# HGRN2 scan and SiLU MLP in one kernel: two w_out pieces staged in w_in's staging tiles, and 38 more idle matmuls in the opening

## The chip, the cores and the metric

The kernel runs on one core of a Trainium2 chip. The metric is the device time of one execution in microseconds (us). Before the change the median of 7 runs is 189.18 us (188.8 to 190.96).

A core has five engines that run side by side and wait for one another by semaphores: TensorE (PE, matmuls; its weight loads are listed apart as PEld), VectorE (DVE), ScalarE (ACT), GpSimd (POOL) and SyncE (SP), which here only issues DMA transfers. Each engine works through its own instructions in order.

## The reference

For 4 batches, 8 heads, 768 steps and a head size of 48, a gated linear attention is computed as a recurrence, and its output goes through a two-layer network with SiLU (model width 384, inner width 2048):

```python
f = 1.0 / (1.0 + np.exp(-f_logit))
for t in range(S):
    state = f[:, :, t, :, None] * state + np.einsum('bhd,bhe->bhde', k[:, :, t], v[:, :, t])
    y[:, :, t] = np.einsum('bhd,bhde->bhe', q[:, :, t], state)
x = y.transpose(0, 2, 1, 3).reshape(B * S, H * D)
h = x @ w_in
out = (h * (1.0 / (1.0 + np.exp(-h)))) @ w_out
```

All inputs and the output are float32 in HBM.

## The kernel before

The 768 steps are cut into 6 chunks of 128, which with 4 batches gives 24 units; a unit is one chunk of one batch with all 8 heads (128 rows of 384 values). Two successive units form a pair. Loads of f, k, q and v bring one unit at a time for the first four units and a pair at a time after that (L485).

A unit goes through these steps. ACT turns f into a logarithm of the gate (e and lf, L492 and L494). PE sums it along the chunk by a triangular matrix (cs, L565 and L569). ACT takes exponentials of the sums (ia, a, al, L572 to L576). POOL and DVE scale k and q by them (L578 and L582, tile qk). PE transposes both (tq, L588), DVE copies them out (L590), PE forms the scores (sc, L599), DVE masks them (L603), PE forms y from scores, v and the running state (L608, L612), DVE casts it (L616), and PE transposes it (L620) into xT. From unit 12 on for q and k, and from unit 15 on for y, DMA transposes replace those on PE. The state is brought forward by L630 (PE), L635 or L637 (DVE) and L641 (POOL). For the network, PE multiplies w_in with xT (m1 for the first 6 units one by one, L529, four blocks j = 0 to 3 of 12 matmuls each; mi for pairs later, L540), ACT applies SiLU into hT (L526, L536), PE multiplies hT with w_out (mo, L551), DVE copies the result (L554 to L559) and a DMA stores it (L562). ACT reloads its function table (L677) whenever it goes from exponentials to SiLU or back.

The weights come in as float32 and are cast to bfloat16 once. w_in is loaded in four pieces into the four staging tiles `ws` (L505), w_out in four pieces into the two staging tiles `wt` (L510), each piece 768 KB with the same number of bytes per partition. A cast (L515 to L520) takes each piece into its place: of w_in, pieces 0, 1 and 2 on POOL and piece 3 on DVE; of w_out, piece 0 and 3 on POOL, 1 on DVE and 2 on ACT. Piece m of w_out is needed by the m-th mo of a unit.

The order on every engine is written out ahead of time. `make_tasks` lists all tasks with durations, priorities and the buffers that they take; `schedule` plays them through a model of the engines and the DMA queue, and the order that comes out is emitted as it stands, with waits added for buffers and data. A buffer is handed from one task to the next by class and slot, and the dictionary `where` (L475 to L478) holds the tile that each task's buffer became.

SP's order in the opening, from its thirteenth load on, is: w_in piece 1, f, w_in piece 2, w_out piece 1, w_in piece 3, k, w_in piece 0, q, w_out piece 0, w_out piece 3, v, f (pair 2), w_out piece 2, and then k, q and v of pair 2 and the loads of the next pairs. The staging tiles of w_in are used once each, in the order of these loads: piece 1 lies in the first, piece 0 in the fourth. Of the two tiles `wt`, one holds w_out piece 1 and then piece 3, the other piece 0 and then piece 2, so the loads of pieces 3 and 2 wait for the casts of pieces 1 and 0.

`idle` looks for gaps of PE in the planned order up to 60 us, and fills each to 75% with matmuls of a zero tile, `blank`, into an idle accumulator bank (`warm`, L652); they compute nothing that is used. The count for a gap is worked out in one line:

```python
n = int(best[0] * cfg["idle_fill"] / (0.0565 if out else 0.113))
```

Of the kernel before, what the change touches and what calls it, by code (L numbers as in the profile page):

```python
# [38 lines left out]
    idle_to=60.0,  # L39
    idle_gap=0.2,  # L40
    idle_fill=0.75,
    hold_exp=0,
    hold_silu=1.23,
    keep_exp=161.0,
# [331 lines left out]
def planned(cfg, slots):  # L376

    tasks, T = make_tasks(cfg)
    schedule(tasks, slots, cfg, cfg["margin"])
    fixed = {e: sorted([t for t in tasks if t.eng == e], key=lambda t: (t.start, t.idx)) for e in ENGINES}  # L380
    schedule(tasks, slots, cfg, 0.0, fixed=fixed)
    order = sorted(tasks, key=lambda t: (t.start, t.idx))
    return order, idle(order, slots, cfg)


def idle(order, slots, cfg):

    held = {s: [] for s in range(slots["mlp"])}
    banks = {}
    for t in order:  # L390
        for x in t.acq + t.use:
            if x.cls == "mlp":
                lo, hi = banks.get(x, (t.start, t.end))
                banks[x] = (min(lo, t.start), max(hi, t.end))
    for x, (lo, hi) in banks.items():
        held[x.slot].append((lo, hi + 0.3))
    out, prev = [], cfg["idle_from"]
    for t in [t for t in order if t.eng == "PE"]:
        lo, hi = prev, t.start - cfg["idle_gap"]
        prev = t.start + t.dur  # L400
        if t.start > cfg["idle_to"]:
            break
        best = (0.0, 0.0, 0)
        for s, spans in held.items():
            a = max([lo] + [e for b, e in spans if b < hi])
            if hi - a > best[0] + 1e-6:
                best = (hi - a, a, s)
        n = int(best[0] * cfg["idle_fill"] / (0.0565 if out else 0.113))
        if n > 0:
            out.append((best[1], best[2], n))  # L410
    return out
# [3 lines left out]
def kernel(  # L415
# [15 lines left out]
    d_model, d_ff = moe_w_in.shape  # L431
# [14 lines left out]
        ws=([128, KT, d_ff // CFG["w_pieces"][0]], F32), wt=([128, NT // CFG["w_pieces"][1], d_model], F32),  # L446
# [12 lines left out]
    NI, NO = CFG["w_pieces"]  # L459
# [15 lines left out]
    where = {}  # L475
    for t in tasks:
        for x in t.acq + t.use:
            where[x.key] = buf[x.cls, x.slot]  # L478
    at = lambda *key: where[key]

    def load(x, us):
# [226 lines left out]
```

## Time and profile before

| what | us |
|---|---|
| median of 7 runs (lowest, highest) | 189.18 (188.8, 190.96) |
| the profiled execution | 188.94 |
| its span, from the first to the last instruction | 187.1 |
| PE busy between 9.88 and 20.0 / 20.0 and 30.0 | 8.22 of 10.12 / 6.54 of 10.00 |
| PE busy between 30.0 and 41.3 | 11.30 of 11.30 |
| mean granted clock of PE | 1.000 |

The profile comes from one execution, and its times count from the span's start. A line of a timeline gives start, length, engine, code line, operation, the tile written and the tiles read, shapes, the number of instructions merged, and in brackets the idle time of the engine before it with what ended it. SPq is SP's queue: a line there is the issue of a DMA, whose length is the time that the issue took, and not that of the transfer; the transfer lands later. The chain of work follows the last instruction back to what released it, step by step.

Six lines of the table of DMA issues give the sizes, and the median time from issue to landing:

| load | count | KB each | us to landing |
|---|---|---|---|
| ws from w_in | 4 | 768 | 8.8 |
| wt from w_out | 4 | 768 | 8.0 |
| f, pair | 10 | 384 | 5.5 |
| k, pair | 10 | 384 | 6.1 |
| q, pair | 10 | 384 | 5.8 |
| v, pair | 10 | 384 | 5.3 |

### The profile page before, as it was taken

The page shows a single profiled execution, that of the slowest core. Times are in us where ns is not written, and L with a number is a line of the kernel's source. Part 1 is how long each engine was busy: PE and PEld are TensorE (multiplying, and loading weights), DVE is VectorE, ACT ScalarE, POOL GpSimd, SP SyncE. Part 2 cuts the span into 40 slices and gives each one's busy share as a digit, 9 for nine tenths or more (in the row PEclk, how much of TensorE's full clock was granted, in tenths as well). Part 3 has the DMA queues.
Part 4 walks back from the last instruction along what each step waited for, and adds up shares of the span by engine and source line. Part 5 has one row for each costly group of instructions (what it writes and reads, how often), then busy time and mean ns, then how long its engine had stood idle before and what let it go on. Part 6 is the DMA issues. An engine that isn't in the chain of part 4 may idle for free.

```text
span 187.1 us, 4875 instructions
## 1 busy us (share of the span) xinstructions
PE 174.3 (93%) x2005; PEld 139.3 (74%) x2005; DVE 95.7 (51%) x185; ACT 131.1 (70%) x217; POOL 70.6 (38%) x112
## 2 busy tenths in 40 slices
PE   5998766999999999979999999999999999999991
PEld 4976656777878879768787786678688886966960
DVE  4269435435877773565527736875542415261011
ACT  4443844998797898998988788668669996810810
POOL 2337628444637470552751642490352006000000
PEclk9999999999999999999999999999999999999999
DMA  6999999899999998998999599488776666413101
GB/s 115 220 205 360 373 356 299 238 222 216 223 224 242 190 253 193 230 245 169 226 142 208 126 178 208 80 126 219 158 154 152 141 130 135 100 25 105 42 16 68
DMA packets 120390, 34.22 MB, mean 183 GB/s; under 512 B 116129, under 2 KB 117793, under 8 KB 120369
## 3 DMA queue, kind: packets, MB, share of 16 engines
q1 hardware_dynamic: 119664, 31.76, 77.8%
q0 software_dynamic: 704, 2.16, 3.2%
q8 instruction: 15, 0.25, 0.6%
q14 instruction: 7, 0.05, 0.1%
HBM read 25.17 MB, written 4.72 MB: 160 GB/s over the span
## 4 chain that ended last, share of the span: by engine, by line
PE 70%; SPq 11%; DMA 7%; ACT 5%; issue 2%; POOL 1%; DVE 1%; DVEq 0%; ACTq 0%
PE mlp L551 29%; PE mlp L540 24%; DMA q<-in_q_dram 7%; SPq L485 7%; SPq L505 4%; PE mlp L529 4%; PE sc L599 3%; PE yd L612 2%; PE yd L608 2%; PE cs L565 2%; ACT L677 2%; PE tq L588 1%; PE yd L630 1%; ACT hT L536 1%; PE tq L620 1%
## 5 line engine op out<-in xcount | busy, mean ns | idle before, releaser
L551 PE MATMUL mlp<-w_out,hT 128*128 128x384 bf16 x384 | 69.9, 326 | 0.0
L536 ACT ACTIVATE hT<-mlp 128x512 bf16<-128x512 f32 x72 | 41.7, 597 | 17.4 <-PE mlp L540 14.9
L540 PE MATMUL mlp<-xT,w_in 128*128 128x256 bf16 x432 | 51.5, 273 | 1.1 <-ACT hT L536 1.0
L551 PEld LDWEIGHTS <-hT 128*128 128x128 bf16 x384 | 34.8, 97 | 19.5
L540 PEld LDWEIGHTS <-w_in 128*128 128x128 bf16 x432 | 46.3, 114 | 3.2 <-issue 1.3
L578 POOL TENSOR_TENSOR qk<-k,ia 128x384 bf16<-128x384 f32 x24 | 24.0, 1001 | 51.1 <-ACT al L576 31.2
L603 DVE TENSOR_TENSOR atm<-sc,triu 128x512 bf16<-128x512 f32 x48 | 30.9, 685 | 19.3 <-PE sc L599 19.3
L677 ACT ACT_TABLE_LOAD x23 | 29.5, 1283 | 0.4
L641 POOL TENSOR_TENSOR st<-sd,al 48x192 bf16<-48x192 f32 x40 | 20.9, 522 | 16.1 <-DVE sd L635 8.7
L572 ACT ACTIVATE ia<-cs 128x384 f32<-128x384 f32 x24 | 11.8, 490 | 15.4 <-PE cs L569 10.5
L559 DVE COPY o<-mlp 128x384 f32<-128x384 f32 x22 | 12.2, 556 | 18.0 <-PE mlp L551 14.1
L616 DVE CAST yb<-yd 128x384 bf16<-128x384 f32 x24 | 13.3, 554 | 15.8 <-PE yd L612 15.8
L529 PE MATMUL mlp<-xT,w_in 128*128 128x128 bf16 x288 | 18.7, 220 | 2.0 <-DVE w_in L520 1.6
L582 DVE TENSOR_TENSOR qk<-q,cs 128x384 bf16<-128x384 f32 x24 | 13.2, 550 | 13.8 <-ACT cs L574 8.7
L529 PEld LDWEIGHTS <-w_in 128*128 128x128 bf16 x288 | 16.9, 114 | 2.8 <-DVE w_in L520 1.8
L526 ACT ACTIVATE hT<-mlp 128x512 bf16<-128x512 f32 x24 | 13.6, 597 | 6.8 <-PE mlp L529 6.4
L580 POOL CAST vb<-v 128x384 bf16<-128x384 f32 x24 | 11.6, 506 | 11.0 <-DMA v<-in_v_dram 10.9
L492 ACT ACTIVATE e<-f 128x768 f32<-128x768 f32 (+1 forms) x14 | 10.5, 747 | 5.9 <-DMA f<-in_f_logit_dram 5.8
L635 DVE TENSOR_TENSOR sd<-yd,st 128x384 f32<-128x384 f32 x16 | 8.9, 555 | 8.3 <-PE yd L630 6.2
L574 ACT ACTIVATE cs<-cs 128x384 f32<-128x384 f32 x24 | 11.4, 477 | 0.6
L652 PE MATMUL mlp<-blank 128*128 128x128 bf16 x112 | 10.6, 266 | 1.0 <-DVE blank L657 1.0
L494 ACT ACTIVATE lf<-e 128x768 bf16<-128x768 f32 (+1 forms) x14 | 10.5, 750 | 0.3
(43 smaller groups left out, 149.6 us busy)
## 6 DMA issues: line engine op xcount, KB each, us to landing
f<-in_f_logit_dram SPq DMA_DIRECT2D x10, 384.0 KB, 5.5
k<-in_k_dram SPq DMA_DIRECT2D x10, 384.0 KB, 6.1
q<-in_q_dram SPq DMA_DIRECT2D x10, 384.0 KB, 5.8
v<-in_v_dram SPq DMA_DIRECT2D x10, 384.0 KB, 5.3
ws<-in_moe_w_in_dram SPq DMA_DIRECT2D x4, 768.0 KB, 8.8
wt<-in_moe_w_out_dram SPq DMA_DIRECT2D x4, 768.0 KB, 8.0
out_dram<-o SPq DMA_DIRECT2D x13, 192.0 KB, 2.1
out_dram<-o POOLq DMA_DIRECT2D x11, 192.0 KB, 3.7
```

The lines of the kernel that those rows point to most:

```text
L485: nc.sync.dma_start(out=dst, in_=SRC[x].rearrange("b h s d -> s (b h) d")[c * C:(c + 1) * C, b * H:(b + n) * H])
L526: return nc.scalar.activation(at("hT", P)[:, 4 * j:4 * j + 4, i * C:(i + 1) * C], h, AF.Silu)
L529: nc.tensor.matmul(h[:, r, :], w_tile(kk, 4 * j + r), at("xT", P)[:, kk, i * C:(i + 1) * C], start=(kk == 0), stop=(kk == KT - 1))
L536: return nc.scalar.activation(at("hT", P)[:, 2 * j:2 * j + 2, :], h, AF.Silu)
L540: nc.tensor.matmul(h[:, i, :], w_tile(kk, n), at("xT", P)[:, kk, :], start=(kk == 0), stop=(kk == KT - 1))
L551: nc.tensor.matmul(o, at("hT", P)[:, n, i * C:(i + 1) * C], w_rows(n), start=(n % (NT // 2 if half else NT) == 0), stop=(n == NT - 1 or ha ...
L578: nc.gpsimd.tensor_mul(at("qk", u)[:, 1, :, 0:D], at("k", P)[:, i], at("ia", u))
L582: nc.vector.tensor_mul(at("qk", u)[:, 0, :, 0:D], at("q", P)[:, i], at("cs", u)[:, 0:HD].rearrange("p (h d) -> p h d", d=D))
L603: nc.vector.tensor_mul(at("atm", u)[:, r], at("sc", u)[:, r], triu[:, None, :].to_broadcast([C, NP, C]))
L616: nc.vector.tensor_copy(at("yb", u), at("y", u))
L641: nc.gpsimd.tensor_mul(at("st", u)[lo:lo + D, :, r * D:(r + 1) * D], at("sd", u)[lo:lo + D, :, r * D:(r + 1) * D], at("al", u)[lo:lo + D, ...
L677: nc.scalar.preload_act_table_set(SETS[after[t.idx]])
```

## The change

Two things are changed. First, after the plan is made and the tiles are assigned, w_out pieces 2 and 3 are given other staging tiles: piece 2 is staged where w_in piece 0 lay, and piece 3 where w_in piece 1 lay, both read with the same bytes in another shape. The order on every engine stays as it was. The load of piece 3 now waits for the cast of w_in piece 1 in place of that of w_out piece 1, and the load of piece 2 for the cast of w_in piece 0 in place of that of w_out piece 0. The casts of both pieces read from the new tiles.

Second, two groups of idle matmuls grow: the group ahead of the cs of unit 3 from 6 to 20, and the one ahead of the block j = 3 of m1 of unit 0 from 2 to 26. PE gets 38 matmuls and 38 weight loads more; no other instruction is added or removed.

```diff
@@ CFG
     idle_fill=0.75,
+    idle_more={'cs_3': 14, 'm1_0_3': 24},
     hold_exp=0,
@@ idle
         n = int(best[0] * cfg["idle_fill"] / (0.0565 if out else 0.113))
+        n += cfg["idle_more"].get("_".join(map(str, t.name)), 0) if n else 0
         if n > 0:
             out.append((best[1], best[2], n))
@@ tile_hgrn2_outer__then__act_silu_kernel
             where[x.key] = buf[x.cls, x.slot]
+    for n in range(2, NO):
+        where["wt", n] = where["ws", n - 2].rearrange("p k n -> p (k n)").rearrange("p (n d) -> p n d", d=d_model)
     at = lambda *key: where[key]
```

## The prediction

> **What bounds the kernel now.** I read the page first (busy shares and granted clock), then TensorE's waits, its timeline through the opening, the queue of SyncE (SP), the chain that ended last, and windows over the same stretch.
>
> The page gives TensorE (PE) as the fullest engine, at the full clock in every slice:
>
> ```profile
> PE 174.3 (93%) x2005; PEld 139.3 (74%) x2005; DVE 95.7 (51%) x185; ACT 131.1 (70%) x217; POOL 70.6 (38%) x112
> ...
> PEclk9999999999999999999999999999999999999999
> ```
>
> Its waits over the whole span (total, times, longest):
>
> ```profile
> PE mlp L529 <- DVE w_in L520: 1.6, 1, 1.6
> PE tq L588 <- DVE qk L582: 1.4, 1, 1.4
> PE mlp L540 <- ACT hT L536: 1.0, 1, 1.0
> ```
>
> The first two lie before 29.52 us, the third at 82.56. After 29.52 that third one is the only wait above a tenth of a microsecond: windows give PE 11.30 busy of 11.30 us from 30.0 to 41.3, 40.11 of 40.20 to 81.5, and 100.67 of 100.80 from 82.6 to 183.4. So the kernel is an opening of 29.5 us set by loads, and then a nearly solid row of matmuls. Only two things can shorten it: an earlier start at 29.52, or the little that is left between matmuls after it.
>
> PE's timeline in the opening (start, length, line, count, idle before):
>
> ```profile
> 18.19 0.50 PE L652 MATMUL mlp<-blank 128*128 128x128 bf16 x6
> 19.45 0.32 PE L565 MATMUL cs<-lf,triu 128*128 128x384 bf16 x1 [0.76 <-ACT lf L494]
> ...
> 23.63 0.28 PE L652 MATMUL mlp<-blank 128*128 128x128 bf16 x2
> 25.54 0.86 PE L529 MATMUL mlp<-xT,w_in 128*128 128x128 bf16 x12 [1.63 <-DVE w_in L520]
> ...
> 29.52 0.62 PE L588 MATMUL tq<-ident,qk 128*128 128x128 bf16 x8 [1.45 <-DVE qk L582]
> ```
>
> The idle matmuls of the change go into the first two bracketed waits. The third, at 29.52, stays as it is: it ends when q, issued at 21.11, lands at 28.82. Every SP issue up to 21.64 stands before the changed ones, so I expect the same landing.
>
> SP's queue, with the two re-staged w_out loads (the second of the x2, and the one at 32.66):
>
> ```profile
> 21.64 3.75 SPq L510 DMA_DIRECT2D wt<-in_moe_w_out_dram  x2
> 25.43 0.43 SPq L485 DMA_DIRECT2D v<-in_v_dram  x1
> 25.91 2.03 SPq L485 DMA_DIRECT2D f<-in_f_logit_dram  x1
> 32.66 0.42 SPq L510 DMA_DIRECT2D wt<-in_moe_w_out_dram  x1
> ```
>
> SP stands from 27.94 to 32.66, because the tile it wants is read until then by the cast in GpSimd (POOL). The chain shows what follows:
>
> ```profile
> 32.66 0.42 SPq L510
> 33.12 1.32 SPq L485
> 34.48 6.18 DMA q<-in_q_dram
> 40.66 0.03 issue
> ...
> 40.78 0.57 DVE qk L582
> 41.35 0.04 issue
> 41.39 0.32 PE cs L565
> ```
>
> The chain puts the late q load on the path. But just before 41.39 PE issued eight L551 matmuls from 39.84, which at 163 ns each (1.30 us for x8 in the chain) run to 41.14. So PE could have started cs 0.25 us earlier, not 6 us; by its idle row only 0.09.
>
> **The change, part by part.**
>
> *14 more idle matmuls before cs_3 (6 become 20).* One costs 57 ns (the x18 group at 14.70: next instruction at 15.72, 1.02 / 18). 20 x 0.057 = 1.13, from 18.19 to 19.32; cs waits for the logarithm until 19.45. Margin 0.13, cost 0.
>
> *24 more before m1_0_3 (2 become 26).* 26 x 0.057 = 1.47, from 23.63 to 25.10; the cast of w_in that the next matmul needs ends at 24.52 + 0.96 = 25.48. Margin 0.44, cost 0. What hides both groups is the wait for the w_in cast, and behind it the 1.45 us before 29.52. At half clock (the 23 idles at 5.35 take 2.41 us, 105 ns each) the groups would last 2.1 and 2.7 us and delay PE by 0.84 and 0.82; 0.38 + 1.63 + 1.45 of waits lie behind the first and 1.45 behind the second. Without that cover they would cost up to 0.8 each. What they can bring is bounded by 0 below, and above by clock lost in other executions: one run of the seven is 2.16 above the lowest (190.96 - 188.80). In this trace the clock is 1.00 through all of it and the matmuls after each wait already come every 57 ns (x12 at 25.54, next at 26.23). I take 0, the value of the profiled row.
>
> *A rule about that.* The Trainium skill ("TensorE: Matmul & The Clock Gate", Part 1) says the clock falls to half only after a whole window of some 3.4 us without activity. It speaks against the idle matmuls: by it no wait here would be long enough in any execution, and the sum stays at 0 for them. The profiled clock agrees (longest wait 1.63 us, 1.00 throughout); no run here shows a longer one. If the repeats' excess were clock loss all the same, dropping the two high repeats (190.06, 190.96) would move the median of the remaining five to 188.94.
>
> *w_out piece 3 goes to the tile of w_in piece 1.* Its issue stops waiting for DVE's cast (22.40 + 0.96 = 23.36) and waits for POOL's cast of w_in, 17.54 + 1.47 = 19.01. It was issued at 24.55 behind the previous issue, which ended at 24.43. So neither wait decides: 0.
>
> *w_out piece 2 goes to the tile of w_in piece 0.* The two POOL casts in question, the one that frees the tile after the change and the pair of which the first frees it before:
>
> ```profile
> 28.08 1.46 POOL L520 CAST w_in<-ws 128x1536 bf16<-128x1536 f32 x1 [1.67 <-DMA ws<-in_moe_w_in_dram]
> ...
> 31.16 3.06 POOL L520 CAST w_out<-wt 128x1536 bf16<-128x1536 f32 x2
> ```
>
> The first cast waits for its own w_in load, which lands at 28.03. SP goes on at about 28.08 + 1.46 + 0.03 = 29.57 instead of 32.66: 3.1 us. Behind it wait the loads of k, q, v, f for the next pairs, and nothing else; the outputs of this stretch are issued by POOL. DMA cannot use all of the 3.1:
>
> ```profile
> 28.00:32.00 4.00, 2.55 (x47) 2.29 (x46) 1.86 (x4) 1.68 (x3) 3.31 (x4) 1.00 1.11 327
> 32.00:35.00 3.00, 3.00 (x43) 2.55 (x42) 1.14 (x2) 2.31 (x5) 2.56 (x3) 1.00 0.72 156
> 35.00:39.00 4.00, 4.00 (x48) 2.83 (x46) 2.31 (x5) 3.96 (x5) 0.90 (x2) 1.00 1.02 268
> ```
>
> (Last two columns: DMA share, GB/s.) Only 32 to 35 us is slack, 0.72 between 1.11 and 1.02: 3 x (1 - 0.72/1.02) = 0.9 to 3 x (1 - 0.72/1.11) = 1.05 us of transfer time. So the loads land some 1.0 us earlier (bounds 0 and 3.1): q at 39.7 instead of 40.66, DVE's qk done near 40.35, and PE's cs starts at 41.14. Gain 0.25, bounds 0 and 0.25. Later loads keep a lead until their own buffers bind; no later PE wait is ended by a load. The 1.0 at 82.56 follows ScalarE (ACT), busy without a break from 74.31 to 82.5, starting from PE's own matmul; it moves along with PE.
>
> *The readers.* The ACT cast of piece 2 starts at 37.52, right behind lf, as its data (37.47) lands; an earlier landing leaves it behind lf. The POOL cast of piece 3 follows its landing at 32.69 as before. 0 each.
>
> **Sum.** 0 + 0 + 0 - 0.25. On the profiled execution (188.94; span 187.1 and 1.8 around it) this is 188.7. That execution is 0.24 below the median of the seven, 189.18, so for the median: 189.18 - 0.25 = **188.9 us**.
>
> **The rivals.**
>
> *The lead is won in full (faster).* The chain is right, the late q load sets the end, and all of the 1.05 us comes off: 189.18 - 1.05 = 188.1. For it: 7.4% of the span is put down to q loads on the path. Against: PE has work without a gap until 41.14. Cleaner repeats through the idle matmuls would go the same way, by at most the 0.38 from median to lowest.
>
> *The early w_out load delays f (slower).* Place: between 29.6 and 34.7 us. Before, SP's stand keeps the 768 KB of piece 2 away from the v and f loads; now it is in the queue with them. If transfers share instead of following in order, f (landing 25.91 + 8.8 = 34.7) comes later by 1.96 (the spacing of the two w_out landings, 30.73 and 32.69) to 2.73 (34.74 to 37.47). ACT takes f at 35.89, so its e, lf, cast, ia and the next table load come 0.85 to 1.6 later, and PE at 42.10 needs the bank that ACT's hT at 41.25 frees, with about 0.25 to spare: +0.6 to +1.35, 189.8 to 190.5, I take 190.3. It passes 0.5% when f lands after about 37.1. For it: DMA is full there. Against: in this trace landings keep the order of issue (28.03, 28.82, 30.73, 32.69, 33.25, 34.74).
>
> *Nothing happens.* SP's new wait ends no earlier, or PE's 0.25 returns before 82.56: 189.2.
>
> **How the numbers follow.** Forecast 0.45 (188.9; own range 188.6 to 189.5), nothing 0.09 (189.2), full lead or cleaner repeats 0.26 (188.1), f delayed 0.20 (190.3). 0.5% of 189.18 is 0.95 us, about what a measurement of this kernel can tell from no change; so faster (below 188.2) 0.26, same 0.54, slower (above 190.1) 0.20. The range reaches to both outer cases: 187.9 to 190.4.
>
> **What would show it.** In the changed profile: w_out piece 2 issued near 29.6 and no SP stand to 32.7; the DMA share from 32 to 35 us near 1.0; q landing near 39.7; PE's cs right behind L551 without the 0.09; PE's waits of 0.76 and 1.63 replaced by idle matmuls while L529 still starts at 25.54 and tq at 29.52; the wait near 82.3 still 1.0. I am wrong if the start at 29.52 moves, if ACT waits for f near 35.9, or if the granted clock differs.

## The result, and the profile after

The changed kernel takes 189.92 us (median of 27 runs, 189.03 to 190.96); the kernel before, beside it on the same chips, 189.97 (64 runs). The ratio is 1.0007, 95% interval 0.9992 to 1.0021. The profiled execution took 189.55 us, its span 187.6. The forecast gain of 0.25 us isn't there. The forecast was 188.9, and 0.79 of the 1.0 us between it and the result comes from the starting value: the median of seven, 189.18, lay that far below the median of 64. The profile of before is of one of the quicker executions of its kernel (188.94), so the 0.5 us between the two profiles is not the difference of the kernels.

In the lines that follow line numbers are 4 higher than in the kernel before: 514 loads w_out, 524 casts, 533 is m1, 569 cs, 586 qk, 592 tq, 656 the idle matmuls. In the kernels of the experiments they differ from these by a few lines more or less, and the tiles named in each line say which step it is. PE's row of the page, the clock by slice, and the three waits that answer to those shown of before:

```profile
PE 176.4 (94%) x2043; PEld 141.3 (75%) x2043; DVE 95.7 (51%) x185; ACT 131.3 (70%) x217; POOL 70.5 (38%) x112
...
PEclk9999999999999999999999999999999999999999
```

```profile
PE mlp L533 <- DVE w_in L524: 1.2, 1, 1.2
PE mlp L544 <- ACT hT L540: 1.0, 1, 1.0
...
PE tq L592 <- DVE qk L586: 0.8, 1, 0.8
```

PE's timeline in the opening of the changed kernel (start, length, line, operation, count, idle before):

```profile
18.01 1.28 PE L656 MATMUL mlp<-blank 128*128 128x128 bf16 x20
19.12 0.33 PE L569 MATMUL cs<-lf,triu 128*128 128x384 bf16 x1
...
23.48 1.61 PE L656 MATMUL mlp<-blank 128*128 128x128 bf16 x26
26.31 0.86 PE L533 MATMUL mlp<-xT,w_in 128*128 128x128 bf16 x12 [1.21 <-DVE w_in L524]
...
29.69 0.62 PE L592 MATMUL tq<-ident,qk 128*128 128x128 bf16 x8 [0.84 <-DVE qk L586]
```

Both groups fit into their waits, as worked out (behind the first cs follows 1.11 after its start), and PE still waits for the cast of w_in and for q. The solid row starts 0.17 later than before (29.69 against 29.52), because q landed at 28.98 and not 28.82.

SP's queue from the issue ahead of w_out piece 2 on:

```profile
26.25 1.83 SPq L489 DMA_DIRECT2D f<-in_f_logit_dram  x1
29.74 3.99 SPq L514 DMA_DIRECT2D ws<-in_moe_w_out_dram  x1
33.77 0.43 SPq L489 DMA_DIRECT2D k<-in_k_dram  x1
34.25 3.42 SPq L489 DMA_DIRECT2D q<-in_q_dram  x1
```

Piece 2 is issued at 29.74 (forecast: near 29.6), but the issue now lasts 3.99 us and ends at 33.73; before, it was issued at 32.66, took 0.42 and ended at 33.08. SP stands as long as before, inside the issue and no longer ahead of it. So the loads behind it are not earlier: k is issued at 33.77 (before 33.12). The stretch that was to fill, 32 to 35 us (time in it, busy time of PE, PEld, DVE, ACT and POOL with counts, clock, DMA share, GB/s):

```profile
32.00:35.00 3.00, 3.00 (x43) 2.61 (x44) 1.29 (x2) 2.31 (x5) 2.28 (x3) 1.00 0.74 132
```

The DMA share is 0.74 where it was 0.72. The end of this part of the chain of waits:

```profile
34.25 6.93 DMA q<-in_q_dram
41.18 0.03 issue
...
41.30 0.57 DVE qk L586
41.87 0.04 issue
41.91 0.32 PE cs L569
```

q of pair 2 lands at 41.18 (before 40.66), and cs (of unit 5) starts at 41.91 (before 41.39).

Between the solid row's start and that cs PE loses time in a place of which the prediction said nothing. PE and POOL, before and after:

```profile
33.78 1.46 PE L551 MATMUL mlp<-w_out,hT 128*128 128x384 bf16 x8
35.08 0.36 PE L612 MATMUL yd<-vb,atm 128*128 128x48 bf16 x8
...
34.16 0.51 POOL L580 CAST vb<-v 128x384 bf16<-128x384 f32 x1
```

```profile
33.95 1.46 PE L555 MATMUL mlp<-w_out,hT 128*128 128x384 bf16 x8
35.49 0.36 PE L616 MATMUL yd<-vb,atm 128*128 128x48 bf16 x8
...
33.52 1.47 POOL L524 CAST w_out<-ws 128x1536 bf16<-128x1536 f32 x1 [0.72 <-DMA ws<-in_moe_w_out_dram]
34.93 0.51 POOL L584 CAST vb<-v 128x384 bf16<-128x384 f32 x1
```

w_out piece 3 lands at 33.47 and not 32.69. POOL casts it, and only then casts v (vb), which ends at 35.44 and not 34.67; yd needs vb, and starts 1.54 after the eight matmuls ahead of it, not 1.30. That makes the whole account of the profiled execution: the solid row 0.17 late, this 0.24, the way to the cs of unit 5 0.11, together 0.52 (41.91 - 41.39). From that cs on both take the same 145.7 us to the end of the span.

### The profile page after: what moved, and what is told of

Read it like the earlier page. It is cut to its first block, busy times and chain, and to the rows that moved or that the text cites. A ratio compares the mean times of both kernels' runs of the same rounds, so it can differ in the third digit from the quotient of the medians.

```text
span 187.6 us, 4953 instructions
## 1 busy us (share of the span) xinstructions
PE 176.4 (94%) x2043; PEld 141.3 (75%) x2043; DVE 95.7 (51%) x185; ACT 131.3 (70%) x217; POOL 70.5 (38%) x112
## 4 chain that ended last, share of the span: by engine, by line
PE 70%; SPq 11%; DMA 8%; ACT 5%; issue 2%; POOL 1%; DVE 1%; DVEq 0%; ACTq 0%
PE mlp L555 29%; PE mlp L544 24%; DMA q<-in_q_dram 8%; SPq L489 7%; PE mlp L533 4%; SPq L509 4%; PE sc L603 3%; PE yd L616 2%; PE yd L612 2%; PE cs L569 2%; ACT L681 2%; PE tq L592 1%; PE yd L634 1%; ACT hT L540 1%; PE tq L624 1%
## 5 line engine op out<-in xcount | busy, mean ns | idle before, releaser
L584 POOL CAST vb<-v 128x384 bf16<-128x384 f32 x24 | 11.6, 504 | 10.1 <-DMA v<-in_v_dram 7.9
L496 ACT ACTIVATE e<-f 128x768 f32<-128x768 f32 (+1 forms) x14 | 10.5, 747 | 5.3 <-DMA f<-in_f_logit_dram 5.3
L656 PE MATMUL mlp<-blank 128*128 128x128 bf16 x150 | 12.7, 253 | 1.0 <-DVE blank L661 1.0
L656 PEld LDWEIGHTS <-blank 128*128 128x128 bf16 x150 | 11.3, 117 | 1.2 <-DVE blank L661 1.0
```

The costliest lines, as they stand in the source:

```text
L656: nc.tensor.matmul(buf["mlp", bank][:, 0:C], blank, blank, start=True, stop=True, skip_group_check=True)
```

## The experiments

They were run in four sets, each beside its own runs of the kernel before: medians 189.95 (29 runs), 190.35 (29), 189.88 (35) and 189.88 (33). Ratios are to those; they are estimated over the runs, and needn't be the quotient of two medians. Unless it says otherwise, an edit is against the changed kernel. "The clock low" stands for an execution whose mean granted clock is under 0.9935; one stretch of 3.4 us at half clock takes 0.5 x 3.4 / 188 = 0.009 off that mean.

### The two halves of the change

**e1_stage**, the staging alone:

```diff
-    idle_more={'cs_3': 14, 'm1_0_3': 24},
+    idle_more={},
```

> The re-staging of w_out pieces 2 and 3 alone, without the added idle matmuls. Theory of the prediction (lead): the load of piece 2 is issued near 29.6 us in place of 32.7, q of pair 2 lands some 1.0 us earlier relative to the load before it, cs follows without its wait, and the time falls by 0.25 us (ratio 0.9987). Theory queue (from the profile after): the issue starts near 29.7 but lasts some 4 us, until the f load before it has drained, so that it ends where it ended before (33 to 33.7); ratio 1.000, within 0.15%.

Measured: 189.94, ratio 1.0005 [0.9975, 1.0035].

**e2_idle**, the idle matmuls alone:

```diff
-    for n in range(2, NO):
-        where["wt", n] = where["ws", n - 2]. ...
```

> The 38 added idle matmuls alone, with the staging of before. Cover theory: they fill waits that end on a cast and on a load, tq still starts when q has landed (28.8 to 29.0), and the ratio is 1.000 within 0.15%. Rival: they delay cs_3 or m1_0_3 and with them the end, by up to 0.8 us each (ratio up to 1.008); other rival: they keep a clock that falls in other executions, 0.3 us off or more (ratio 0.998 or below), with a higher granted clock than before.

Measured: 190.04, ratio 1.0009 [0.998, 1.0038]. Neither half moves the time by more than these intervals of some 0.3%, and no large gain of the one hides a large loss of the other.

### Why SP's earlier start brought nothing

**e3_early**, piece 2 in the tile of w_in piece 2, whose cast is done long before, and no more idle matmuls:

```diff
+    idle_more={},
...
-        where["wt", n] = where["ws", n - 2]. ...
+        where["wt", n] = where["ws", 4 - n if n == 2 else 1]. ...
```

> Piece 2 is staged where w_in piece 2 lay (free from 22.0 us) in place of piece 0's tile (free at 29.6), no idle matmuls added: SP waits for no cast at all between 21 and 37 us. Lead theory: the issue starts near 28.1, the load lands near 35.7, the DMA share from 32 to 35 us rises from 0.72 towards 1.0, time -0.25 us. Queue theory: the issue starts near 28.1, lasts 5 to 6 us, ends near 33.5, DMA share from 32 to 35 us stays near 0.74, ratio 1.000 within 0.15%.

Measured: 190.00, ratio 1.0008 [0.9975, 1.0041]. SP's queue:

```profile
27.46 1.92 SPq L489 DMA_DIRECT2D f<-in_f_logit_dram  x1
29.47 5.09 SPq L514 DMA_DIRECT2D ws<-in_moe_w_out_dram  x1
34.60 0.92 SPq L489 DMA_DIRECT2D k<-in_k_dram  x1
```

With no cast to wait for at all, SP goes straight on behind f and stands 5.09 us in the issue.

**e8_drop_wo2** takes the load itself away (piece 2 never comes in, and its cast reads w_in piece 0):

```diff
+        if t.name == ("wo", 2):
+            return
         if kind == "wo":
```

> The change with the load of w_out piece 2 (the re-staged one) left out; its cast reads w_in piece 0 in its place. The k, q, v, f loads behind it come 1.9 to 2.7 us earlier, more than any re-staging can bring. Prediction's bound: PE has work without a gap until its matmul before cs of unit 5, so the end moves by 0.25 to 0.5 us at most (0.25 in before, 0.37 in the profile after; ratio 0.998 to 0.9987). Rival (the chain is right): the late q load is on the path in full, 1.9 us or more off (ratio 0.990).

Measured: 189.88, ratio 0.998 [0.9953, 1.0008]. q of pair 2 landed at 39.22 and PE no longer waited ahead of cs, yet the ratio is at most half a per cent under 1. That agrees with the bound of 0.25 us on this wait, and not with the 6 us that the chain of waits gives to the q load. The issue of k, next in line, lasted from 28.35 to 33.98: with no w_out load there at all, SP stands until the same time. So what holds it is the queue, and neither the tile nor the load that is next.

**g1_pool_queue** takes the load off SP's queue:

```diff
+    t = next(t for t in tasks if t.name == ("wo", 2))
+    tasks.remove(t)
+    tasks.insert(1 + [t.name for t in tasks].index(("ci", 0)), t)
...
-            return nc.sync.dma_start(...)
+            return (nc.gpsimd if m == 2 else nc.sync).dma_start(...)
```

> The changed kernel, with one transfer moved: the load of w_out piece 2 is issued by GpSimd (POOL), directly behind its cast of w_in piece 0, and no longer by SP. Theory queue: a load on SP's queue is taken only as earlier loads of that queue drain, so the freed wait only became a long issue. Then on POOL's own queue piece 2 is on its way near 30 us, lands at 36.5 or earlier (37.80 in the changed kernel), the DMA share from 32 to 35 us rises from 0.74 to 0.9 or more, and k of pair 2 takes the long issue instead, to about 34. Theory engines: the 16 DMA engines themselves are held up by the loads in flight. Then piece 2 lands at 37.3 to 38.3 all the same and the share stays at 0.7 to 0.8. The time by both: 189.5 to 190.1, ratio 0.998 to 1.001, since at most 0.25 us of TensorE's work waits for these loads.

Measured: 190.82, ratio 1.0052 [1.0026, 1.0078]. Windows of this kernel (columns as above):

```profile
32.00:35.00 3.00, 3.00 (x49) 2.62 (x46) 1.29 (x2) 2.33 (x4) 2.90 (x3) 1.00 1.16 319
35.00:39.00 4.00, 4.00 (x36) 2.39 (x34) 2.31 (x5) 2.39 (x4) 1.01 (x3) 1.00 0.68 151
```

Each of the two theories is half right. The DMA share from 32 to 35 us rises from 0.74 to 1.16, so the DMA engines had room, and SP's queue had kept the load from using it. But the load landed at 37.71, as in the changed kernel (37.80) and as the other theory had it, because it shared the engines with the loads in flight. k took over the long issue (5.53 us, to 33.97), q of pair 2 landed at 41.18 as in the changed kernel, and the share from 35 to 39 us fell from 1.03 to 0.68. The time, which both had as unchanged, got longer. ACT's timeline shows where it went:

```profile
35.05 1.28 ACT L684 ACT_TABLE_LOAD   x1
37.89 0.85 ACT L499 ACTIVATE e<-f 128x768 f32<-128x768 f32 x1 [1.56 <-DMA f<-in_f_logit_dram]
38.77 0.84 ACT L501 ACTIVATE lf<-e 128x768 bf16<-128x768 f32 x1
```

f now lands at 37.87, and ACT starts on it at 37.89 (before 35.89). PE waits 0.67 for the logarithm at 39.66 and 0.45 for hT at 43.90:

```profile
39.66 0.32 PE L572 MATMUL cs<-lf,triu 128*128 128x384 bf16 x1 [0.67 <-ACT lf L501]
...
43.90 1.50 PE L536 MATMUL mlp<-xT,w_in 128*128 128x128 bf16 x24 [0.45 <-ACT hT L533]
```

Together 1.12, and 190.82 - 189.88 = 0.94 came. This is the rival in which an early w_out load delays f, at 190.3 by its price; on one queue it did not come about (f landed at 35.33 in the changed kernel), on two it did.

### What the idle matmuls do

**e4_more**, 64 more in the second group, too many for its wait:

```diff
-    idle_more={'cs_3': 14, 'm1_0_3': 24},
+    idle_more={'cs_3': 14, 'm1_0_3': 88},
```

> The change with 88 in place of 24 more idle matmuls ahead of block 3 of m1: 90 x 57 ns = 5.1 us from 23.5, to 28.6, where L529 started at 25.5 (before) or 26.3 (after). Cover theory: PE comes 2.3 to 3.1 us late to that block, 0.84 to 1.45 of it are absorbed by the wait for q, tq starts at 31.1, and as PE is solid from there the end moves by the same 1.4 to 1.6 us (ratio 1.0075). Rival (later waits absorb a delay): the end moves by 0.4 us or less (ratio up to 1.002).

Measured: 192.18, ratio 1.0141 [1.0091, 1.0191], some 0.7% or 1.3 us more than expected. A delay ahead of the solid row does pass through to the end. Its profile shows a surplus in two places. The group itself starts at 24.78, 1.30 later than in the changed kernel, so that the solid row starts at 32.15 and not at 31.1. And there are waits behind it:

```profile
PE mlp L544 <- DMA xT<-yb: 1.2, 1, 1.2
...
PE tq L592 <- DVE xT L626: 0.6, 1, 0.6
```

Neither is there in the changed kernel. The profiled execution was its slowest (193.57), so how the surplus of the median divides is not shown.

**e5_noidle**, no idle matmuls after 14 us of the plan, 51 fewer than in the changed kernel (groups of 5, 20 and 26; the group of 18, which the expectation counts too, is still there):

```diff
+    idles = [x for x in idles if x[0] < 14.0]
```

> The change without any idle matmul after 14 us of the plan: the last 69 are gone (18, 5, 20 and 26), those up to 14 us stay. Cover theory: they hide no work and hold no clock, so ratio 1.000 within 0.2% and a granted clock of 1.00 from 20 to 30 us. Clock rival: the clock falls to half for some 3 us between 15 and 33 us; each us of it behind 29.5 costs half a us (ratio 1.005 or more).

Measured: 190.31, ratio 1.0003 [0.9973, 1.0033]. The clock was low in 12 of 12 executions. Windows of 3.4 us of its profile:

```profile
15.80:19.20 3.40, 1.39 (x22) 1.02 (x20) 2.26 (x5) 0.29 (x1) 2.36 (x3) 1.00 1.03 327
19.20:22.60 3.40, 2.56 (x28) 2.17 (x28) 1.29 (x2) 2.60 (x6) 1.53 (x2) 0.50 1.00 382
22.60:26.00 3.40, 3.40 (x40) 3.40 (x38) 1.77 (x2) 1.92 (x4) 1.73 (x3) 0.50 1.09 355
```

The clock goes to half after a stretch in which PE was busy 1.39 us of 3.40. The same in e1_stage:

```profile
24.00:27.50 3.50, 1.21 (x22) 1.04 (x20) 1.79 (x3) 1.04 (x3) 0.84 (x1) 1.00 1.13 342
27.60:31.00 3.40, 3.40 (x37) 3.40 (x35) 1.38 (x3) 1.54 (x3) 1.93 (x3) 0.50 1.02 398
```

e1_stage's longest wait in the opening was 2.29 us. There the drop costs: it holds PE busy until 31.0, past the landing of q at 29.41, and its x12 groups take 1.44 and 1.48 us in place of 0.83. In e5_noidle it lies before 26.0, and PE waited 1.58 ahead of the solid row all the same.

How often the clock was low, and the median of the executions with and without it:

| kernel | low | with | without |
|---|---|---|---|
| before, four sets | 72 of 126 | 190.26, 190.66, 190.26, 190.11 | 189.66, 190.01, 189.50, 189.31 |
| changed | 3 of 28 | 190.16 | 189.85 |
| e1_stage | 8 of 12 | 190.16 | 189.36 |
| e2_idle | 5 of 12 | 190.68 | 189.63 |
| e5_noidle | 12 of 12 | 190.31 | none |

So the kernel before did lose clock, in 57% of its executions; its one profile shows none. Those are 0.6 to 0.8 us longer. The change brings them down to 11%, worth (0.57 - 0.11) x 0.7 = 0.3 us if nothing else moved. The same idle matmuls with the staging of before (e2_idle) still lost clock in 5 of 12. The 0.3 isn't seen in the time. The change's executions without a drop have 189.85, against 189.57 for all 54 such of before; but by set those lie between 189.31 and 190.01, so that this alone doesn't show them to be slower. f4_tiny, further down, shows it better.

**e6_none**, no idle matmuls at all, and **f2_before_none**, the same edit in the kernel before:

```diff
+    idles = []
```

> The change without any idle matmul at all (150 fewer). Measures what those of the first 14 us hold. Cover theory: the clock rises later than 9.7 us, matmuls take 105 ns instead of 57 for longer, but loads set the start at 29.5; ratio up to 1.003 if the clock is up by 29.5. Clock rival: PE is busy too little before 29.5 for the clock to rise, and some us of the solid row run at half clock: 1.5 us or more (ratio 1.008 or more).

> The kernel before without any idle matmul, staging of before. With the same without idle matmuls after the change (ratio 0.9962) it shows whether the staging is worth anything once the idle matmuls are gone: queue theory says no, ratio 0.996 within 0.2%; lead theory says that it loses 0.25 us, ratio 0.9975 or more.

Measured: 189.39, ratio 0.9962 [0.9938, 0.9986], and 189.35, ratio 0.9971 [0.9943, 0.9998]. Both are a little faster than the kernel before, though f2_before_none's interval only just leaves 1 out. PE's timeline in e6_none:

```profile
21.35 4.03 PE L534 MATMUL mlp<-xT,w_in 128*128 128x128 bf16 x36
...
27.50 0.83 PE L534 MATMUL mlp<-xT,w_in 128*128 128x128 bf16 x12
...
29.27 0.62 PE L593 MATMUL tq<-ident,qk 128*128 128x128 bf16 x8
```

Up to 25.4 us PE runs at half speed (36 matmuls in 4.03 us, 112 ns each, against 57); from 27.5 on it is at full speed. The granted clock of its windows says 1.00 all the way, so this half speed, from the start on, isn't in the table above, which counts the later drops. It still reaches the solid row at 29.27, 0.25 ahead of the kernel before: the cover of the opening is large enough for half clock all the way. In this one profile the lead is lost again: the cs of unit 5 waits 0.75 for q of pair 2 and starts at 42.00. Between them the two kernels show the staging again at about nothing (0.9962 against 0.9971, the intervals overlap).

### What the instructions of the idle matmuls cost

The profile lists a queue that fetches instructions. In the trace each fetch is 16 KB, comes after about every 256th instruction of PE (in the changed kernel after 201, 521, 757, 989), and keeps one DMA engine for 0.9 to 1.3 us. A load is spread over 16 engines and has landed only when its last part has. When a fetch falls among loads, one part can come late. Times in us, each row from one profiled execution (of f1_long its slowest, 191.67); "late" is the last part behind the one before it:

| kernel | ratio | clock low | first fetch | q of unit 2 late | q of unit 3 late | fetch near 32 | w_out piece 3 late |
|---|---|---|---|---|---|---|---|
| before | 1 | 72 of 126 | 12.3 | 1.43 | 0.77 | 33.0 | 0.71 |
| changed | 1.0007 | 3 of 28 | 11.3 | 0.49 | 1.00 | 31.3 | 1.56 |
| e1_stage | 1.0005 | 8 of 12 | 11.6 | 0.54 | 0.55 | 33.7 | 0.54 |
| e2_idle | 1.0009 | 5 of 12 | 11.6 | 0.78 | 0.80 | 32.0 | 1.23 |
| e3_early | 1.0008 | 5 of 12 | 10.5 | 1.20 | 1.27 | 33.9 | 1.28 |
| e5_noidle | 1.0003 | 12 of 12 | 11.9 | 1.30 | 0.92 | 33.9 | 0.94 |
| e6_none | 0.9962 | 0 of 12 | 23.7 | 0.15 | 0.02 | 33.3 | 0.07 |
| f2_before_none | 0.9971 | 1 of 12 | 23.8 | 0.23 | 0.19 | 32.7 | 0.18 |
| f1_long | 1.002 | 1 of 12 | 18.5 | 0.22 | 0.08 | 31.8 | 1.45 |
| f4_tiny | 1.001 | 0 of 12 | 10.6 | 1.06 | 0.63 | 31.6 | 1.04 |
| g3_same_count | 0.9966 | 0 of 11 | 16.5 | 0.21 | 0.62 | 33.2 | 0.13 |

The change's 76 extra instructions of PE (38 matmuls and their weight loads) bring the third fetch from 33.0, where the DMA engines have room (share 0.71 from 33 to 34 us), to 31.3, where they are full (1.08 from 28 to 32). The lag of w_out piece 3 is 1.04 to 1.56 in the four kernels with a fetch from 31.3 to 32.0. But a fetch there isn't the only way to it: in e3_early and e5_noidle the part is 1.28 and 0.94 late with none near it, and there the lag of the first fetch seems to stay with its engine from load to load. In the other five it is 0.07 to 0.71. The three rows with a gain have neither a lag over 0.2 at this load nor, but for one execution, a low clock.

What this lag costs can be followed in two profiles. All parts but the last of w_out piece 3 had landed at 31.9 in the changed kernel and at 32.0 in the one before; the last part makes the 33.47 against 32.69, and with it the 0.24 us ahead of yd that were shown above. In f1_long the piece lands at 34.86, and the same wait is long enough to be listed:

```profile
36.88 0.36 PE L616 MATMUL yd<-vb,atm 128*128 128x48 bf16 x8 [1.39 <-POOL vb L584]
```

In f4_tiny and e2_idle yd starts 1.44 and 1.35 after the matmuls ahead of it, in the three kernels with a gain 1.30 as before.

**f4_tiny** keeps the number of idle matmuls and cuts each to one column and one row of output:

```diff
-            nc.tensor.matmul(buf["mlp", bank][:, 0:C], blank, blank, ...)
+            nc.tensor.matmul(buf["mlp", bank][0:1, 0:1], blank[:, 0:1], blank[:, 0:1], ...)
```

> The change with its 150 idle matmuls cut to one column of weights and one column moved: the instruction count of the change, hardly any TensorE time. Theory fetch: first fetch near 11 us as with the change, one DMA engine late by 0.5 us or more at q of unit 2, ratio 1.000 to 1.004 (no clock kept either). Theory activity: as without idle matmuls, ratio 0.996 and the loads as early as there.

Measured: 189.98, ratio 1.001 [0.9982, 1.0038]. With next to no work in them the idle matmuls cost the same. No execution had the clock low, and yet it is slower than the executions without a drop of the kernel before in its set (189.50, 16 of them). PE ran at half speed until 23.6 us, as without any.

**f1_long** turns it round, a quarter of the number and each four times as wide:

```diff
-        for _ in range(n):
-            nc.tensor.matmul(buf["mlp", bank][:, 0:C], blank, blank, ...)
+        for _ in range((n + 2) // 4):
+            nc.tensor.matmul(buf["mlp", bank], blank[:, 0:C], blank, ...)
...
-        blank = sb.tile([C, C], BF16, name="blank")
+        blank = sb.tile([C, 4 * C], BF16, name="blank")
```

> The change with its idle matmuls four times as wide (128x512) and a quarter as many: 39 in place of 150, so TensorE is kept about as busy with 222 fewer instructions. Theory fetch: what the idle matmuls cost is a 16 KB instruction fetch in the opening (near 11 to 12 us in every trace with them, near 24 without), which makes one DMA engine late (last of the 16 parts of a load 0.5 to 1.4 us behind the 15th, 0.15 without); then the first fetch moves to 18 us or later, the last part of q of unit 2 is within 0.3 of the 15th, q of unit 3 lands some 0.5 us earlier and the ratio is 0.996 to 0.998. Theory activity: it is the matmuls themselves (or the clock that they raise early) that cost; then the ratio is 1.000 within 0.15%.

Measured: 190.21, ratio 1.002 [0.9991, 1.0049]: the fetch theory in its plain form (fewer instructions, less time) fell here. The first fetch did move, to 18.5, but the next came at 31.8, and w_out piece 3's last part was 1.45 late. From this came the theory that the places of the fetches count and not their number.

**g3_same_count** tests that. It keeps the change's two groups and takes out 38 idle matmuls from 5 to 10 us, so that PE has as many instructions as before the change:

```diff
+    idles = idles[:1] + idles[3:]
```

> The changed kernel without the second and third groups of idle matmuls (23 and 15, from 5.2 to 10 us), so that it has as many instructions on TensorE as the kernel before, and keeps the two groups that the change enlarges. Theory fetch: the third fetch of TensorE's instructions falls back from 31.3 to 33 us, out of the busy stretch, the last part of w_out piece 3 lands within 0.7 us of the one before it, and the time comes down to a ratio of 0.996 to 0.9985. Theory count: only the presence of idle matmuls in the opening matters and not where the fetches fall; ratio 0.9995 to 1.0015.

Measured: 189.48 (188.74 to 189.90, 11 runs), ratio 0.9966 [0.9936, 0.9995]; the clock low in 0 of 11. The third fetch is back at 33.2. Its window from 32 to 35 us and the start of the solid row:

```profile
32.00:35.00 3.00, 3.00 (x44) 2.55 (x43) 1.22 (x2) 2.31 (x5) 2.62 (x3) 1.00 0.96 196
```

```profile
29.59 0.62 PE L593 MATMUL tq<-ident,qk 128*128 128x128 bf16 x8 [0.57 <-DVE qk L587]
```

The DMA share there is 0.96 (0.74 in the changed kernel), and PE's wait ahead of the solid row 0.57 (0.84). With the change's two groups, and as many instructions as before, the gain that the change lacks is there, though the two intervals (0.9936 to 0.9995, and 0.9992 to 1.0021) just overlap. The gain is that of the clock: the executions without a drop of the kernel before have 189.31 in this set, no more than g3_same_count's 189.48. That is what a kernel would show that keeps the clock and doesn't pay for it. The first fetch moved too (11.3 to 16.5), so which of the two fetches matters more isn't settled. Nor is another reading ruled out: f4_tiny takes away the work of the idle matmuls and f1_long most of the instructions, neither gains, and the kernels that gain take away some of both.

### What else bounds the opening

**e7_drop_wo1** leaves out the load of w_out piece 1 (it never comes in, and its cast reads w_in piece 1):

```diff
+    where["wt", 1] = where["ws", 1]. ...
...
+        if t.name == ("wo", 1):
+            return
```

> The change with the load of w_out piece 1 (768 KB, issued ahead of w_in pieces 3 and 0 and q of unit 3) left out; its cast reads w_in piece 1 in its place. The loads behind it come some 1.9 us earlier. If the start at 29.5 sets the end: w_in piece 3, piece 0 and q of unit 3 land 1.9 us earlier, tq starts near 27.7, and the end comes 1.5 to 1.9 us earlier (ratio 0.991) provided the loads of pair 2 come earlier by as much. If PE's row is held elsewhere (ACT, a later load): less than 0.5 us (ratio above 0.997).

Measured: 188.08, ratio 0.9886 [0.9844, 0.9929]; q landed at 27.79, 1.03 earlier than in the kernel before. So the bytes loaded in the opening cost time. Where the 2.3 us are won the profile doesn't show: it is of the slowest of the six executions (188.81), with the clock at half from 21.3 to 24.7, and its solid row starts at 29.58, no earlier than before.

**f3_wo1_late** brings the same load in later instead, with no idle matmuls:

```diff
+    idles = []
+    for a, b in ((("wo", 1), ("wo", 0)), (("co", 1), ("qkc", 3))):
+        t = next(t for t in tasks if t.name == a)
+        tasks.remove(t)
+        tasks.insert(1 + [t.name for t in tasks].index(b), t)
```

> The change without idle matmuls, and with the load of w_out piece 1 moved behind that of piece 0 (its cast on DVE behind the qkT copy of unit 3), so that w_in pieces 3 and 0 and q of unit 3 are loaded 768 KB earlier. If only the start at 29.5 sets the end: q lands 1.9 us earlier and the ratio falls to 0.987. If the bytes up to q of pair 2 (41 us) are a second bound, since none of them is saved: the start moves by 1.5 us or more and the wait before cs of unit 5 grows by as much; ratio 0.994 to 0.997, no more than 0.3 us better than without idle matmuls alone.

Measured: 189.61, ratio 0.997 [0.9939, 1.0001]. q landed at 26.67, and the solid row started 1.3 us earlier than before, but it isn't solid any more:

```profile
34.51 0.36 PE L621 MATMUL yd<-vb,atm 128*128 128x48 bf16 x8 [0.58 <-POOL vb L589]
41.26 0.32 PE L574 MATMUL cs<-lf,triu 128*128 128x384 bf16 x1 [0.53 <-DVE qk L591]
```

A second bound lies close behind the first: the bytes up to q of pair 2, which landed at 40.53, 0.13 from where it was.

**g2_none_pool** (no idle matmuls, w_out piece 2 on POOL's queue) and **g4_late_pool** (both of these, and piece 1 late):

```diff
+    idles = []
...
+            return (nc.gpsimd if m == 2 else nc.sync).dma_start(...)
```

> As the kernel before this one, and without any idle matmuls. Theory queue: 189.1 to 189.4, ratio 0.995 to 0.997 (0.9962 was measured without idle matmuls and with the load on SP's queue), with the load's landing ahead of 36.5. Theory engines: the same time within 0.1%, landing near 37.5.

> No idle matmuls, w_out piece 1 loaded behind piece 0 and cast behind the copy of qkT of unit 3, and w_out piece 2 issued by GpSimd directly behind its cast of w_in piece 0. Without the last of these three the opening ended 1.4 us earlier but new waits of 0.58 and 0.53 us took most of it back (ratio 0.997). Theory queue: piece 2 off SP's queue lets q of pair 2 land by 39.5, the wait near 41.3 falls under 0.2, and the ratio is 0.993 to 0.995. Theory engines: bytes up to q of pair 2 are what counts, q lands near 40.5 again, the ratio is 0.9965 to 0.9985.

Measured: 190.19, ratio 1.001 [0.9982, 1.0037], and 191.02, ratio 1.0055 [1.0021, 1.009]; both expectations missed. Piece 2 landed at 37.70 and 36.69. As in g1_pool_queue it takes its place from the loads in flight: in g4_late_pool v, whose last part came at 36.35, and PE stood for its cast (wait, total, times, longest):

```profile
PE yd L624 <- POOL vb L592: 2.5, 1, 2.5
```

## Why the prediction failed

The step that failed is the lead of the loads behind w_out piece 2: forecast 0.25 us of gain, measured 0, because the wait ahead of the issue came back as a longer issue. Two terms put at 0 were not 0 either: what the idle matmuls bring and cost, and the reader of w_out piece 3. The terms one by one:

**Cover of the idle matmuls: right.** Both groups ended inside their waits, 0 paid on the path. e4_more shows the price once the cover is gone: 2.2 us by its median, where 1.4 to 1.6 were expected with the start of the group as it was.

**What the idle matmuls bring, taken as 0: off by some 0.3 us on either side.** The profiled row showed the clock at 1.00 and I took that for the kernel's rule; 57% of its executions did lose clock. The change nearly ends that. What it brings (0.3 by the table) isn't left in the time. g3_same_count, which differs from the changed kernel only in the 38 idle matmuls taken out from 5 to 10 us, has the gain (0.9966). That ties the loss to PE's instructions ahead of the loads, by intervals that just overlap; that it works through the late parts of the loads is read from the traces (0.24 us in the profiled execution) and was not varied by itself. Nor is it shown that a drop of the clock is the cause of the slower executions: late loads make long waits, which can bring both the drop and the time. e1_stage's profile shows a drop that costs, e5_noidle's and e6_none's show half clock under cover.

**w_out piece 3, 0, and its reader, 0: the first right, the second not.** It was issued at 25.37, behind the previous issue as before, so neither tile decides. But "the POOL cast of piece 3 follows its landing at 32.69 as before" took the landing for granted. It came at 33.47, and with POOL's cast of v behind it this delayed PE by 0.24 us in the profiled execution, as much as the whole forecast gain.

**w_out piece 2: the step that failed.** "So the loads land some 1.0 us earlier (bounds 0 and 3.1)", "Gain 0.25". The start at 29.57 was right (29.74). But I took the slack of the DMA engines for room that the next load could use, and the length of an issue (0.42) as fixed. The issue lasts until the queue has room: 3.99 us here, 3.55 in e1_stage, 5.09 in e3_early, where it began without any wait. In the profile of before, the line at 21.64 with 3.75 us for two issues showed such lengths already, and its issue of piece 2, short as it was, ended at 33.08, 0.39 after w_out piece 3 had landed: the wait for the cast stood in front of a wait for the queue of about the same end. The term measured 0: q of pair 2 landed 0.52 later, not 1.0 earlier. Its upper bound agrees with e8_drop_wo2, where q of pair 2 landed 1.44 earlier than before and the ratio is 0.998.

**The rivals.** "Nothing happens" is what came, by another way than either that I gave: the wait became an issue, and what the clock brought was lost elsewhere. The lead in full is answered by e8_drop_wo2: a lead of 1.44 us at q brings a ratio of 0.998, 0.9 us at the most. The rival of the delayed f was rightly held back by the order of landings on one queue; g1_pool_queue shows its price, 0.94, where that order is given up.

**A rule that did not hold.** The windows of e5_noidle and e1_stage show the clock falling after 3.4 to 3.5 us in which PE was busy 1.39 and 1.21 us. The Trainium skill ("TensorE: Matmul & The Clock Gate", Part 1) lets the clock fall after a whole idle window of about 3.4 us. The length of the half-clock stretches, 3.4 us or twice that, agrees with the page; the condition, read as a window without any matmul, doesn't, and the measurement decides.

## What to carry to other kernels

A wait for a buffer that stands ahead of a DMA issue is worth removing only if the queue behind it has room: look at the lengths of the issues around it, and read a long one as a wait. Filler instructions that cost no time on their engine still have to be fetched, and the fetch is one more transfer among the loads; count them, and look at where the fetches fall. A load that nothing seems to wait for can still hold up an engine that works in order, and what stands behind it there: follow its reader's next task too. One profile doesn't show what happens in half of the executions: read the clock of each run before a term of the clock is set to 0.

## What was not expected of the hardware

The granted clock falls to half with PE 35 to 41% busy in a stretch of 3.4 to 3.5 us, with no wait over 2.3 us in it (e1_stage, e5_noidle).

The fetch of PE's instructions is part of the traffic: 16 KB keep one DMA engine for about 1 us. The Trainium skill ("Runtime: NRT & Kernel Launch", Instruction fetch mechanics) gives the same 16 KiB blocks of 256 instructions and calls their cost mostly hidden. No listed wait of PE in the changed kernel is put down to instructions, which agrees with it, but the last part of a load in flight came up to 1.56 us behind the others (w_out piece 3 in the changed kernel).

The issue of a load on SP's queue can last 3.5 to 7.0 us (6.98 for k in g4_late_pool). Around 33 us it ends 0.3 to 0.6 us after w_out piece 3, issued three places earlier, has landed: 33.73 behind 33.47 in the changed kernel, 34.56 behind 34.19 in e3_early, 33.08 behind 32.53 in e6_none, and for k in e8_drop_wo2, with no piece 2 on the way, 33.98 behind 33.66. g4_late_pool is an exception: k's issue there ended at 36.18, 2.0 after piece 3 had landed.

Two queues share the DMA engines: piece 2 on POOL's queue had its share from 32 to 35 us, and f, issued 3.8 us earlier on SP's, landed at 37.87 (35.33 in the changed kernel).
